# Spectral filter plus MLP on one core: load order, activation table, first tile and schedule changed together

## The chip, the cores and the metric

The kernel runs on one core of one Trainium2 chip. The metric is device time in microseconds, the median of several runs. All times below are in microseconds. The engines are PE (matrix multiply; PEld is its weight load), DVE (vector), ACT (scalar, activation functions), POOL (general) and SP, which here only issues DMAs.

## What is computed

```python
x  = A_x                                   # 1 x 2048 x 640, bf16
xn = (x - mean(x)) / sqrt(var(x) + 1e-5)   # over the last axis
A  = irfft2(rfft2(xn) * (w_r + 1j * w_i))  # filter 2048 x 321
B  = gelu(xn @ w1 + b1) @ w2 + b2          # w1 640 x 1536, w2 1536 x 640, tanh form
return x + A + B
```

## The kernel before

The 2048 rows are 16 tiles of 128 partitions. Both branches start from the normalised rows and meet in one sum at the end.

- **Normalise** (all sixteen tiles): DVE takes two BNStats per tile (L567), an aggregate (mv, L569) and adds epsilon (ve, L571); POOL raises to the power -0.5 (rstd, L572); DVE forms -mean x rstd (nmr, L574) and writes the normalised tile (L595).
- **Transposes**: PE turns each normalised tile with five identity matmuls (L607) into one PSUM bank; DVE or ACT copies it to xnT.
- **First layer**: per block of 1, 1, 2, 2, 2, 4 and 4 tiles and per slice of 128 of the 1536 hidden columns, five matmuls (W by xnT) fill one of the PSUM banks 4 to 7; ACT applies the GELU (L656) and writes gT. W1 is loaded in three parts (W1P).
- **Spectral branch**: DVE folds each pair of tiles (L618, L622), PE multiplies it with gtab, ACT copies to XV; then etab (32- and 128-row matmuls), the small matmuls with mtab, the products with the filter Wf on DVE (T and Z, L723, L727), the small matmuls with ntab, DMA transposes on SP (L748), getab, folds on DVE, htab.
- **Second layer**: per tile 24 matmuls with W2. For the eight tiles in KEEP the second layer is done early into PSUM, DVE adds b2 (b2bc, the bias on all partitions, L824), and POOL adds x by an accumulating DMA (L826). For the others ACT copies b2bc to the place (L803), POOL accumulates x there, and the second layer is summed with the last spectral product in PSUM. DVE adds both and SP writes the tile out (L838).

The order on each engine is made when the program is built: `Sched.schedule` plays all operations against estimated durations (`mm_us`, `dve_us`, `act_us`, `pool_us`) and priorities (`PRIO`), and each engine then runs its list in that order. SP's list was the order of the source. Waits are semaphores; an engine stands at the first instruction of its list whose wait isn't met. `CHAIN` fixes the order of the spectral stages among themselves: b (etab), c (mtab), d (ntab). All DMAs of `load` are issued at L469, and all copies from PSUM to SBUF at L485 (ACT) and L486 (DVE), nearly all matmuls at L474.

SP's list before: x and W1 in pieces with ident, b1t and gtab between them, then etab, mtab, ntab, the 34 filter loads of rows of 642 bytes (Wf), W2, getab, htab, b2bc, then the 16 transposes and the 18 stores. The first part of W1 goes out on ACT's queue.

Of the kernel before, what the change touches and what calls it, by code (L numbers as in the profile page):

```python
# [7 lines left out]
BF = dt.bfloat16  # L8
# [89 lines left out]
def act_us(n, ptr=0):  # L98
    return 0.055 + n / 1200.0 + 0.09 * ptr
# [57 lines left out]
class Sched:  # L157
# [36 lines left out]
    def schedule(self):  # L194
# [24 lines left out]
        while left:  # L219
            best = None  # L220
            for e in self.engines:
# [27 lines left out]
                if e == "sp":  # L249
                    t, o = min(cands, key=lambda c: c[1].seq)  # L250
                    if o is not min((p for p in pend[e] if not p.done), key=lambda p: p.seq):
                        continue
                else:
                    t0 = min(c[0] for c in cands)
                    near = [c for c in cands if c[0] <= t0 + 0.03]
                    if e == "pe" and self.mode != "128":
                        near = [c for c in cands if c[0] <= t0 + HOLD and c[1].alts and c[1].alts[0][0][0] == self.mode] or near
                    t, o = min(near, key=lambda c: (-c[1].prio, c[1].seq))
# [13 lines left out]
            if o.nbytes:  # L272
                if e == "pool":
                    o.end = t + 5.0
                else:
                    s = max(t + 0.9, dma_free)
                    dma_free = s + o.nbytes / o.rate
                    o.end = dma_free + 0.9
            else:
                o.end = t + dur + LAT[e]  # L280
# [96 lines left out]
W1P = [(0, 5), (5, 8), (8, 12)]  # L377
# [5 lines left out]
PRIO = {"hps": 10, "gelu": 50, "pb": 70, "pc": 80, "filt": 85, "ipc": 90, "eps": 60, "fin": 40}  # L383
# [4 lines left out]
HOME = (KEEP[:max(0, len(KEEP) - 7)] + tuple(c for c in range(15) if c not in KEEP))[:8]  # L388
WARM = (55, 12)


def bass_parallel_sum__spectral_gfnet__dense_activation_gelu__prompt_kernel(
# [21 lines left out]
    with ExitStack() as es:  # L414
# [27 lines left out]
        nmr = sb("nmr", [128, 16], F32)  # L442
# [25 lines left out]
        def load(dst, src, buf, nbytes, after=(), reads=(), rate=395e3, q="sp"):  # L468
            return K.op([(q, 0.45)], 400, lambda e, _: e.dma_start(dst, src), reads=reads, writes=[buf], after=after, nbytes=nbytes, rate=rate)  # L469
# [20 lines left out]
        K.op([("dve", 0.1)], 300, lambda e, _: e.memset(warm[:], 0.0), writes=[B_warm])  # L490
        K.op([("pool", 0.1)], 100, lambda e, _: e.memset(mhalf[:], -0.5), writes=[B_mh])
# [16 lines left out]
        def load_x(c, n, q="sp"):  # L508
            o = load(view(X, c * D, [[1, n * D]]), xv[:, c:c + n, :].rearrange("p c d -> p (c d)"), B_x[c], n * D * 256, q=q, rate=155e3 if c == 0 else 395e3)
            for i in range(1, n):  # L510
                B_x[c + i].writers.append(o)

        def load_w1(j, q="sp"):
            a, b = W1P[j]
            load(view(W1, 128 * a, [[F, 5], [1, 128 * (b - a)]]), w1v[:, :, 128 * a:128 * b], B_w1s[j], 163840 * (b - a), q=q, rate=300e3)
# [7 lines left out]
        load_w1(2)  # L523
        load(gtab[:], const["G"], B_g, 524288)
        for c in range(4, 16, 2):
            load_x(c, 2)
        load(etab[:], const["E"], B_e, 204800, rate=250e3)
        load(mtab[:], const["M"], B_m, 65536, rate=70e3)
        load(ntab[:], const["N"], B_n, 49152, rate=70e3)
        WP = 32 * KP  # L530

        def load_w(wsrc, p0, off, row, n, step):
            load(bass.AP(tensor=Wf, offset=p0 * WP + off, ap=[[2 * WP, 16], [2 * KP, n], [1, 321]]),
                 bass.AP(tensor=wsrc.tensor, offset=wsrc.offset + row * 321, ap=[[128 * 321, 16], [step * 321, n], [1, 321]]),
                 B_w, 16 * 642 * n, after=[wpad], rate=165e3)
# [12 lines left out]
        load(W2[:], w2v, B_w2, F * D * 2)  # L548
        load(getab[:], const["GE"], B_ge, 204800)
        load(htab[:].rearrange("p a b -> p (a b)"), const["H"], B_h, 524288)  # L550
        load(b2bc[:], bass.AP(tensor=b2v.tensor, offset=b2v.offset, ap=[[0, 128], [1, D]]), B_b2b, 163840)
# [3 lines left out]
        K.op([("dve", 0.08)], 200, lambda e, _: e.tensor_copy(b1col[:], psb(B_b1ps.slot, [[1, NFC]])), reads=[B_b1ps], writes=[B_b1c])  # L555
# [3 lines left out]
        norm_ops, ring_ops, a_ops = [], [], []  # L559
        B_rs = [Buf(f"rstd{c}") for c in range(16)]  # L560
        for c0, n in [(0, 1), (1, 1)] + [(c, 2) for c in range(2, 16, 2)]:
            pr = 100 - c0 / 2
            B_mv, B_ve, B_r = Buf("mv"), Buf("ve"), Buf("r")
            for c in range(c0, c0 + n):
                B_st = Buf("st")
                for h in range(2):
                    K.op([("dve", 0.393)], pr, lambda e, _, c=c, h=h: e.bn_stats(stats[:, c, 6 * h:6 * h + 6], view(X, c * D + H2 * h, [[1, H2]])),  # L567
                         reads=[B_x[c]], writes=[B_st])
                K.op([("dve", 0.119)], pr, lambda e, _, c=c: e.bn_aggr(mv[:, c, :], stats[:, c, :]), reads=[B_st], writes=[B_mv])  # L569
            a, b = c0, c0 + n  # L570
            K.op([("dve", 0.09)], pr, lambda e, _, a=a, b=b: e.tensor_scalar_add(ve[:, a:b], mv[:, a:b, 1], 1e-5), reads=[B_mv], writes=[B_ve])  # L571
            K.op([("pool", 0.65)], pr, lambda e, _, a=a, b=b: e.tensor_tensor(out=rstd[:, a:b], in0=ve[:, a:b], in1=mhalf[:, a:b], op=ALU.pow),  # L572
                 reads=[B_ve, B_mh], writes=[B_r])
            K.op([("dve", 0.071)], pr, lambda e, _, a=a, b=b: e.scalar_tensor_tensor(out=nmr[:, a:b], in0=mv[:, a:b, 0], scalar=-1.0,  # L574
                                                                                     in1=rstd[:, a:b], op0=ALU.mult, op1=ALU.mult),
                 reads=[B_mv, B_r], writes=B_rs[a:b])
            for c in range(a, b):
                B_rs[c].writers += B_r.writers

        for pair in range(8):  # L580
# [10 lines left out]
            for n in range(2):  # L591
# [4 lines left out]
                    out=xnv(n, 0, [[1, D]]), in0=view(X, c * D, [[1, D]]), scalar1=rstd[:, c:c + 1], scalar2=nmr[:, c:c + 1], op0=ALU.mult, op1=ALU.add),  # L596
                    reads=[B_x[c], B_rs[c]], writes=[xn, B_xn])
                norm_ops.append(o)
                if c in BYDMA:
                    K.op([("sp", 1.6)], 0, lambda e, _, c=c, n=n, xnv=xnv: e.dma_start_transpose(xnT[:, :, 128 * c:128 * c + 128], xnv(n, 0, [[1, D]])),  # L600
                         reads=[B_xn, xn], writes=[B_xnT[c]], nbytes=163840, rate=150e3)
                    continue
                tps = Buf(f"tps{c}", psum, 1, ZONE["tps"])

                def xt(e, _, n=n, xnv=xnv, tps=tps):
                    for j in range(5):
                        ins = e.transpose(psb(tps.slot, [[1, 512]]).bitcast(BF)[:, 128 * j:128 * j + 128], xnv(n, 128 * j, [[1, 128]]), ident[:])  # L607
                    return ins
                tp = K.op([("pe", 5 * mm_us(128))], pr, xt, reads=[B_xn, xn, B_id], writes=[tps], alts=[[("128", 5 * mm_us(128))]])
                if not c:  # L610
                    idle(WARM[1], WARM[1] * mm_us(128), gate=[tp])
                K.op([("dve", 0.41), ("act", act_us(640))], pr,
                     copy(lambda c=c: xnT[:, :, 128 * c:128 * c + 128],
                          lambda tps=tps: psb(tps.slot, [[1, 512]]).bitcast(BF)[:, 0:640].rearrange("p (j t) -> p j t", j=5)),
                     reads=[tps], writes=[B_xnT[c]])
# [54 lines left out]
        def five_segs(n):  # L670
            return [("128", 4 * n * mm_us(Q4)), ("32", n * 0.075 + 0.01)]
# [5 lines left out]
        for gi, (c0, n) in enumerate(GROUPS):  # L677
# [8 lines left out]
            for v in range(2):  # L686
                K.op([("dve", dve_us(320 * n) + 0.05), ("act", act_us(320 * n) + 0.16)], PRIO["pb"] - c0 / 10,
# [3 lines left out]
        for P in range(4):  # L691
# [4 lines left out]
            for r in range(2):  # L696
                cps = Buf(f"cps{P}_{r}", psum, 4, ZONE["cps"])
                zone[f"c{P}{r}"] = pe([("small", 2 * mm_us(KP) + 0.06)], PRIO["pc"] - P / 2 + 0.02 * r, lambda P=P, r=r, cps=cps: [
# [31 lines left out]
            for v in range(2):  # L730
                dps = Buf(f"dps{P}_{v}", psum, 4, ZONE["dps"])
                d_ops.append(pe([("small", 2 * mm_us(H2) + 0.06)], PRIO["ipc"] - P / 2 + 0.02 * (1 - v), lambda P=P, v=v, Zs=Zs, dps=dps: [
# [12 lines left out]
            for pair, U, B_u in zip(two, Us, B_us):  # L745
                for qq in range(2):
                    q = 2 * pair + qq
                    K.op([("sp", 1.3)], 0, lambda e, _, q=q, qq=qq, U=U, uv=uv: e.dma_start_transpose(  # L748
                        XV[:, :, 128 * q:128 * q + 128], uv(U, D * qq, [[1, D]])), reads=[U, B_u], writes=[B_v[q]], nbytes=163840, rate=180e3)
# [11 lines left out]
        for gi, (c0, n) in enumerate(GROUPS):  # L761
# [20 lines left out]
            for i in range(n):  # L782
# [38 lines left out]
                if kept:  # L821
                    kps = Buf(f"kps{c}", psum, 2, ZONE["fps"])
                    second(c, kps, 0, D, pr, ([kept_ops[-2]] if len(kept_ops) > 1 else [pb_ops[0]]) + [l1_of[j][-1] for j, (t0, nt) in enumerate(BLOCKS) if t0 <= c < t0 + nt])
# [4 lines left out]
                for o0, w in [(0, D)] if c < 15 else [(0, H2), (H2, Q4), (H2 + Q4, Q4)]:  # L828
# [9 lines left out]
                    last.append(K.op([("sp", 0.35)], 0, lambda e, _, c=c, os_=os_, o0=o0, w=w: e.dma_start(ov[:, c, o0:o0 + w], view(W1, OST + os_.slot * D + o0, [[1, w]])),  # L838
# [33 lines left out]
```

## Time and profile before

| | before |
|---|---|
| median of 3 runs (lowest to highest) | 157.81 (157.73 to 157.98) |
| profiled execution: span, first to last instruction | 160.8 |
| profiled execution: its own time | only the span is given |
| PE busy | 148.7 (92%) |
| DVE, ACT, POOL busy | 113.2 (70%), 84.0 (52%), 26.2 (16%) |
| mean granted PE clock | 0.979 |
| DMA moved | 21.71 MB, mean 135 GB/s |

The span counts from the first to the last instruction of one execution. Busy shares are averages over stages with different limits. A row of a timeline is: start, length, engine, line, operation, out<-in, shape, count, and in brackets the idle time before it with what ended it. A line that ends in q is the engine's queue of issues.

### The profile page before, as it was taken

How to read it: one execution, taken by the hardware profiler on the slowest of the kernel's cores; microseconds unless marked ns; L12 is line 12 of the kernel's file. 1: busy time of each engine (PE TensorE's matmuls, PEld its weight loads, DVE VectorE, ACT ScalarE, POOL GpSimd, SP SyncE). 2: the span in 40 equal slices, each digit the busy share in tenths (PEclk: the TensorE clock that was granted, in tenths of full speed). 3: DMA queues.
4: the chain of work that ended last, by engine and by line, in shares of the span. 5: the costliest groups of instructions: out<-in, count | busy, mean ns of one | idle time of the engine just before them, and what ended most of it. 6: DMA issues, size and time to landing. Idle time of an engine off the chain costs nothing.

```text
span 160.8 us, 4316 instructions
## 1 busy us (share of the span) xinstructions
PE 148.7 (92%) x1823; PEld 98.4 (61%) x1845; DVE 113.2 (70%) x258; ACT 84.0 (52%) x147; POOL 26.2 (16%) x33
## 2 busy tenths in 40 slices
PE   7979999999981999998999999998999999999994
PEld 7969899999850356464465355443447664665563
DVE  1659999999993024589995786991206999998222
ACT  3288989899709655353246884356865451211000
POOL 1112101111027600302113045202006000000000
PEclk9999999999997589999999999999999999999999
DMA  5999995458941940051649509996651914222112
GB/s 143 356 380 394 212 140 121 105 128 202 378 189 20 207 99 4 4 84 34 131 81 161 90 4 156 208 166 126 138 115 18 167 64 161 86 86 82 41 56 66
DMA packets 30394, 21.71 MB, mean 135 GB/s; under 512 B 12712, under 2 KB 28200, under 8 KB 30376
## 3 DMA queue, kind: packets, MB, share of 16 engines
q1 hardware_dynamic: 23320, 15.39, 38.4%
q0 software_dynamic: 6400, 5.24, 20.2%
q10 hardware_dynamic: 656, 0.82, 1.4%
q8 instruction: 14, 0.23, 0.6%
q14 instruction: 4, 0.03, 0.1%
HBM read 13.58 MB, written 2.62 MB: 101 GB/s over the span
## 4 chain that ended last, share of the span: by engine, by line
PE 57%; SPq 22%; DMA 8%; DVE 4%; ACT 4%; issue 3%; DVEq 0%
PE ps L474 57%; SPq L469 22%; DMA b2bc<-in_B_b_dram 6%; DVE T L723 2%; DMA XV<-U 2%; ACT gT L656 2%; ACT Wf L485 1%; DVE Z L727 1%; ACT xnT L803 1%; DVE Y L486 1%; DVEq L359 0%; ACT U L485 0%; DVE X L824 0%; DVE W L835 0%; SPq L748 0%
## 5 line engine op out<-in xcount | busy, mean ns | idle before, releaser
L474 PE MATMUL ps<-xnT,W 128*128 128x256 bf16 (+2 forms) x413 | 57.8, 294 | 6.0 <-ACT gT L656 4.6
L474 PE MATMUL ps<-W,gT 128*128 128x128 bf16 (+3 forms) x382 | 55.2, 292 | 1.6 <-issue 1.3
L474 PEld LDWEIGHTS ps<-xnT,W 128*128 128x128 bf16 x420 | 35.8, 99 | 23.2 <-ACT gT L656 6.3
L656 ACT ACTIVATE gT<-ps,b1col 128x256 bf16<-128x256 f32 (+2 forms) x84 | 39.7, 506 | 8.8 <-PE ps L474 6.8
L474 PEld LDWEIGHTS ps<-W,gT 128*128 128x128 bf16 x396 | 29.8, 98 | 23.3 <-issue 2.4
L826 POOL DMA_DIRECT2D xnT<-in_A_x_dram x8 | 12.3, 1785 | 33.0 <-ACT xnT L803 23.5
L567 DVE BATCH_NORM_STATS2 stats<-X 128x6 f32<-128x320 bf16 x32 | 14.3, 472 | 2.9 <-DMA X<-in_A_x_dram 2.9
L485 ACT ACTIVATE Wf<-ps 128x960 bf16<-128x960 f32 (+1 forms) x9 | 7.6, 878 | 15.5 <-PE ps L474 15.5
L723 DVE TENSOR_TENSOR T<-Y,Wf 128x1288 bf16<-128x1288 bf16 x16 | 12.4, 821 | 0.8 <-issue 0.8
L572 POOL TENSOR_TENSOR rstd<-ve,mhalf 128x2 f32<-128x2 f32 (+1 forms) x9 | 6.3, 699 | 38.1 <-DVE ve L571 38.1
L485 ACT ACTIVATE Xb<-ps 128x960 bf16<-128x960 f32 (+1 forms) x7 | 7.9, 1157 | 8.0 <-PE ps L474 7.8
L826 POOL DMA_DIRECT2D X<-in_A_x_dram x8 | 7.0, 873 | 27.1 <-DVE X L824 25.6
L485 ACT ACTIVATE XV<-ps 128x1280 bf16<-128x1280 f32 (+1 forms) x8 | 9.3, 1157 | 2.9 <-PE ps L474 2.7
L835 DVE TENSOR_TENSOR W<-ps,xnT 128x640 bf16<-128x640 f32 x8 | 6.5, 819 | 5.6 <-PE ps L474 5.4
L485 ACT ACTIVATE Y<-ps 128x644 bf16<-128x644 f32 x8 | 5.7, 707 | 8.5 <-PE ps L474 8.5
L486 DVE CAST Wf<-ps 128x960 bf16<-128x960 f32 (+1 forms) x3 | 3.1, 1044 | 8.6 <-PE ps L474 8.6
L486 DVE CAST Y<-ps 128x644 bf16<-128x644 f32 x8 | 6.6, 825 | 3.6 <-PE ps L474 3.6
L622 DVE TENSOR_TENSOR T<-T 128x512 bf16<-128x512 bf16 (+1 forms) x32 | 8.5, 315 | 0.0
L486 DVE CAST Xb<-ps 128x960 bf16<-128x960 f32 (+1 forms) x5 | 5.5, 1098 | 4.1 <-PE ps L474 4.1
L485 ACT ACTIVATE U<-ps 128x512 bf16<-128x512 f32 (+1 forms) x12 | 4.6, 435 | 7.1 <-PE ps L474 4.6
L835 DVE TENSOR_TENSOR W<-ps,X 128x640 bf16<-128x640 f32 (+2 forms) x10 | 6.7, 683 | 1.9 <-PE ps L474 1.9
L474 PE MATMUL ps<-getab,XV 32*128 32x160 bf16 (+1 forms) x128 | 7.6, 242 | 0.0
(47 smaller groups left out, 147.7 us busy)
## 6 DMA issues: line engine op xcount, KB each, us to landing
xnT<-in_A_x_dram POOLq DMA_DIRECT2D x8, 320.0 KB, 4.9
X<-in_A_x_dram POOLq DMA_DIRECT2D x8, 320.0 KB, 5.1
out_dram<-W SPq DMA_DIRECT2D x15, 160.0 KB, 1.8
X<-in_A_x_dram SPq DMA_DIRECT2D x7, 320.0 KB, 10.2
W<-in_B_w_dram SPq DMA_DIRECT2D x1, 1920.0 KB, 9.7
Wf<-in_A_w_r_dram SPq DMA_DIRECT2D x15, 80.2 KB, 9.3
Wf<-in_A_w_i_dram SPq DMA_DIRECT2D x15, 80.2 KB, 2.6
W<-in_B_w_dram ACTq DMA_DIRECT2D x1, 800.0 KB, 5.2
```

Of the source, the lines that this page charges most:

```text
L469: return K.op([(q, 0.45)], 400, lambda e, _: e.dma_start(dst, src), reads=reads, writes=[buf], after=after, nbytes=nbytes, rate=rate)
L474: ins = e.matmul(o_, lhsT=lw, rhs=rh, start=st, stop=sp_, skip_group_check=True)
L485: return e.activation(dst(), src(), ACT.Copy, scale=scale)
L486: return e.tensor_copy(dst(), src())
L567: K.op([("dve", 0.393)], pr, lambda e, _, c=c, h=h: e.bn_stats(stats[:, c, 6 * h:6 * h + 6], view(X, c * D + H2 * h, [[1, H2]])), reads=[B ...
L572: K.op([("pool", 0.65)], pr, lambda e, _, a=a, b=b: e.tensor_tensor(out=rstd[:, a:b], in0=ve[:, a:b], in1=mhalf[:, a:b], op=ALU.pow), read ...
L622: ring_ops.append(K.op([("dve", dve_us(4 * w, 2))], pr, lambda e, _, op=op, x1v=x1v, xfv=xfv, o_=o_, o0=o0, o1=o1, w=w: e.tensor_tensor(ou ...
L656: K.op([("act", act_us(128 * nt, 1))], pr + PRIO["gelu"], lambda e, _, c0=c0, nt=nt, fc=fc, hps=hps: e.activation(gT[:, fc, 128 * c0:128 * ...
L723: filt_ops.append(K.op([("dve", dve_us(4 * KP, 2))], pr, lambda e, _, k=k, Y=Y, TB=TB, pair=pair: e.tensor_tensor(out=view(TT, TB.slot * 8 ...
L727: K.op([("dve", dve_us(2 * KP, 2))], pr, lambda e, _, TB=TB, Z=Z, r=r, op=op: e.tensor_tensor(out=view(Zb, Z.slot * 4 * KP + r * KP, [[2 * ...
L826: K.op([("pool", 1.5)], 51, lambda e, _, c=c, xov=xov, shaped=shaped: e.dma_start(xov(0, D), shaped(xv[:, c, :]), accum_op=ALU.add), reads ...
L835: K.op([("dve", dve_us(w))], 95, lambda e, _, os_=os_, fps=fps, o0=o0, w=w, xov=xov, shaped=shaped, base=base: e.tensor_tensor(out=shaped( ...
```

## The change

- Loads: tiles 4 and 5 of x go ahead of gtab. W2 (in two halves), b2bc, and by their place in SP's new list also ntab, getab and htab, stand ahead of the 34 filter loads. SP's list is now made by the scheduler too. W1's parts are 3, 4 and 5 slices instead of 5, 3 and 4; the first still goes out on ACT's queue.
- Activation table: the GELU's table is loaded once, as ACT's first instruction, ahead of its W1 load. Copies use the same table. The copy of b1 to b1col moves from DVE to ACT.
- First tile: its transposes go into two banks, three blocks copied by DVE and two by ACT.
- nmr is gone: the tile is normalised as (x - mean) x rstd.
- Tile 1's first statistics wait in the scheduler for tile 0's normalise to start (its second ones don't, and stand ahead of tile 0's epsilon in DVE's list).
- The scheduler's estimates are changed, the first layer's priority is 45 instead of 10, and the early second layers no longer wait for the first etab matmuls. The order comes out anew: on PE, the transposes of a pair stand around the previous pair's gtab matmuls, 24 second-layer matmuls stand ahead of the first etab ones, first- and second-layer work alternates through the spectral stages, and 42 second-layer with 7 first-layer matmuls stand between the last ntab and the first getab matmuls, where 6 and 35 stood. On POOL, accumulating DMAs stand between the later rstd operations. On ACT, the copies of b2bc begin behind the GELUs of the third block, where they began behind those of the fifth.

```diff
 def act_us(n, ptr=0):
-    return 0.055 + n / 1200.0 + 0.09 * ptr
+    return 0.067 + n / 1200.0 + 0.078 * ptr
...
-                if e == "sp":
-                    t, o = min(cands, key=lambda c: c[1].seq)
-                    if o is not min((p for p in pend[e] if not p.done), key=lambda p: p.seq):
-                        continue
-                else:
...
-W1P = [(0, 5), (5, 8), (8, 12)]
+W1P = [(0, 3), (3, 7), (7, 12)]
...
-PRIO = {"hps": 10, "gelu": 50, "pb": 70, "pc": 80, "filt": 85, "ipc": 90, "eps": 60, "fin": 40}
+PRIO = {"hps": 45, "gelu": 50, "pb": 70, "pc": 80, "filt": 85, "ipc": 90, "eps": 60, "fin": 40}
...
+WLATE = 19.0
...
+        K.op([("act", 1.3)], 410, lambda e, _: e.preload_act_table(ACT.Gelu_apprx_tanh), writes=[Buf("table")])
...
+        load_x(4, 2)
         load(gtab[:], const["G"], B_g, 524288)
-        for c in range(4, 16, 2):
+        for c in range(6, 16, 2):
             load_x(c, 2)
-        load(etab[:], const["E"], B_e, 204800, rate=250e3)
-        load(mtab[:], const["M"], B_m, 65536, rate=70e3)
-        load(ntab[:], const["N"], B_n, 49152, rate=70e3)
+        for h in range(2):
+            load(W2[:, 6 * h:6 * h + 6, :], w2v[:, 6 * h:6 * h + 6, :], B_w2, F * D)
+        load(etab[:], const["E"], B_e, 204800, rate=340e3)
+        load(mtab[:], const["M"], B_m, 65536, rate=200e3)
+        load(b2bc[:], bass.AP(tensor=b2v.tensor, offset=b2v.offset, ap=[[0, 128], [1, D]]), B_b2b, 163840)
+        load(ntab[:], const["N"], B_n, 49152, rate=200e3)
...
-                 B_w, 16 * 642 * n, after=[wpad], rate=165e3)
+                 B_w, 16 * 642 * n, after=[wpad], rate=165e3, issue=0.645, late=WLATE))
...
-        load(W2[:], w2v, B_w2, F * D * 2)
         load(getab[:], const["GE"], B_ge, 204800)
...
-        K.op([("dve", 0.08)], 200, lambda e, _: e.tensor_copy(b1col[:], psb(B_b1ps.slot, [[1, NFC]])), reads=[B_b1ps], writes=[B_b1c])
+        K.op([("act", 0.2)], 200, lambda e, _: e.activation(b1col[:], psb(B_b1ps.slot, [[1, NFC]]), ACT.Copy), reads=[B_b1ps], writes=[B_b1c])
...
-                    out=xnv(n, 0, [[1, D]]), in0=view(X, c * D, [[1, D]]), scalar1=rstd[:, c:c + 1], scalar2=nmr[:, c:c + 1], op0=ALU.mult, op1=ALU.add),
+                    out=xnv(n, 0, [[1, D]]), in0=view(X, c * D, [[1, D]]), scalar1=mv[:, c, 0:1], scalar2=rstd[:, c:c + 1], op0=ALU.subtract, op1=ALU.mult),
...
+                if not c:
+                    st_ops[2].gate.append(o)
...
+                for j0, j1, engs in ((0, 3, ["dve"]), (3, 5, ["act"])) if c == 0 else ((0, 5, ["dve", "act"]),):
+                    nj = j1 - j0
+                    tps = Buf(f"tps{c}", psum, 1, ZONE["tps"])
...
-                    second(c, kps, 0, D, pr, ([kept_ops[-2]] if len(kept_ops) > 1 else [pb_ops[0]]) + [l1_of[j][-1] for j, (t0, nt) in enumerate(BLOCKS) if t0 <= c < t0 + nt])
+                    second(c, kps, 0, D, pr, ([kept_ops[-2]] if len(kept_ops) > 1 else []) + [l1_of[j][-1] for j, (t0, nt) in enumerate(BLOCKS) if t0 <= c < t0 + nt])
```

## The prediction

> **What bounds the kernel now.** I read the table of waits first, then the chain that ended last, then PE's timeline with the clock by stretch, and last the head of ACT's and SP's timelines. The page's own first line says PE is busy 92% of the span, so the question is what the missing time and the slow time of PE are.
>
> Waits (who waited for whom: us in all, times, longest):
>
> ```profile
> PE ps L474 <- ACT gT L656: 4.6, 2, 3.9
> ACT xnT L803 <- DMA b2bc<-in_B_b_dram: 4.4, 1, 4.4
> PE ps L474 <- issue: 1.7, 11, 0.2
> PE ps L474 <- DVE xnT L486: 0.7, 2, 0.5
> ```
>
> One wait of 3.9 us is almost half of all that PE waits after it has started. PE's timeline around it, then four stretches (length; busy time and count on PE, PEld, DVE, ACT, POOL; granted clock; DMA share; GB/s):
>
> ```profile
> 47.14 0.44 PE L607 MATMUL ps<-ident,T 128*128 128x128 bf16 x5
> 51.49 5.73 PE L474 MATMUL ps<-xnT,W 128*128 128x512 bf16 x13 [3.91 <-ACT gT L656]
> 57.02 0.78 PE L474 MATMUL ps<-gtab,T 128*128 128x128 bf16 x10
> ```
> ```profile
> 44.00:48.00 4.00, 3.58 (x32) 2.14 (x30) 3.82 (x13) 0.00 (x0) 0.85 (x1) 1.00 0.55 211
> 48.00:52.00 4.00, 0.51 (x2) 0.23 (x3) 1.54 (x6) 3.65 (x7) 2.62 (x2) 0.79 0.05 8
> 52.00:56.00 4.00, 4.00 (x11) 1.41 (x10) 0.00 (x0) 2.52 (x5) 2.67 (x3) 0.50 1.39 204
> 56.00:60.00 4.00, 3.95 (x35) 2.24 (x34) 0.96 (x1) 2.50 (x4) 0.35 (x1) 0.86 0.61 116
> ```
>
> ACT does nothing from 44 to 48: its queue stands at the copy of b2bc (L803), and the GELUs that would free PE's banks stand behind it. When PE comes back the clock is at half. The SP queue says why b2bc is late:
>
> ```profile
> 9.76 14.78 SPq L469 DMA_DIRECT2D Wf<-in_A_w_r_dram  x17
> 24.57 11.81 SPq L469 DMA_DIRECT2D Wf<-in_A_w_i_dram  x17
> 36.43 0.59 SPq L469 DMA_DIRECT2D W<-in_B_w_dram  x1
> 38.53 0.53 SPq L469 DMA_DIRECT2D b2bc<-in_B_b_dram  x1
> ```
>
> The 34 filter loads take SP 26.6 us to issue; b2bc goes out at 38.5 and lands 9.8 us later. Their own user, the product L723, first runs at 69.1.
>
> The head of ACT:
>
> ```profile
> 0.74 0.46 ACTq L469 DMA_DIRECT2D W<-in_B_w_dram  x1
> 6.89 0.70 ACT L485 ACTIVATE xnT<-ps 128x640 bf16<-128x640 bf16 x1 [4.37 <-PE ps L607]
> 7.92 1.28 ACT L656 ACT_TABLE_LOAD   x1 [0.33 <-DVE b1col L555]
> 9.21 2.42 ACT L656 ACTIVATE gT<-ps,b1col 128x128 bf16<-128x128 f32 x8
> ```
>
> PE starts first-layer work at 7.65, fills its four banks, and waits 0.70 at 9.64 for the GELU behind that table load.
>
> **What of the span can move.** The span is 160.8. PE's useful stream runs from 7.65 to 158.43 with idle of 0.70, 0.47, 0.20, 3.91, 1.7 (eleven small ones), 0.36, 0.49 and 0.28: 8.1 in all. Under the slow clock 13 matmuls of 128x512 took 5.53 (51.49 to 57.02); at 0.216 each (35 of them between 112.50 and 120.06) they are 2.81, so 2.7 is lost, and the ten gtab matmuls behind them took 0.83 where 20.34 to 20.90 shows 0.56: 3.0 in all. Start 7.65, idle 8.1, clock 3.0 and the tail of 2.4 are 21.1; the other 139.7 is matmul streaming, and the change keeps its counts (after and before: 120, 180 and 120 first-layer matmuls of width 128, 256 and 512; 396 second-layer ones).
>
> **Part by part.**
>
> *W2, tables and b2bc ahead of the filter loads.* SP's new order has b2bc 19th, at about 0.74 + 18 x 0.48 = 9.4 us (0.47 each in the first rows of the queue). Ahead of it lie 7.5 MB; the stretches 0:4 to 12:16 moved 141, 356, 380 and 393 GB/s, 5.1 MB by 16 us, and 2.4 MB more at 380 is 6.4 us: it lands near 23. ACT reaches its first L803 after the third block's GELUs; before, the matmuls of that block ended at 25.7, so ACT gets there at about 24.5 in the new time. The wait of 3.9 goes, and with it the clock loss of 3.0. What is late next is PE itself: it streams without idle from 16.6 to 47.6 in the profile. W2 lands near 21 and PE first asks for it behind all 256-wide blocks, past 40.
>
> *The filter loads behind them.* Their issue starts at 22 x 0.48 = 11 instead of 9.8, their data behind all that is ahead of them (about 24.5). The 20:36 stretches carry them at 107 to 139 GB/s, so 2.6 MB at 120 is 22 us: about 47. The first product is due near 61. Cost nothing; cover 14 us; past that each us is a us. The transposes that SP issues behind them (81.05 before) are later still.
>
> *One table load, first on ACT.* The 1.28 at 7.92 leaves the path. But it now stands ahead of ACT's issue of the first W1 part, which moves from 0.74 to about 2.05; that part shrinks from 800 to 480 KB (landing 5.2 us after issue before), so it lands between 5.5 and 7.0, before the first matmul. Price if not: up to 1 us. The bias copy goes to ACT ahead of xnT's copy and waits on b1t's DMA, issued 2.13: covered until 6.6.
>
> *First tile.* Chain before: statistics at 3.65, ve at 4.81, rstd 5.05, nmr 5.66, normalise 5.85, transposes 6.41. The new order drops nmr (0.2) but puts a BNStats of tile 1 (0.4) ahead of ve: normalise near 6.05. That one waits for tile 1's x, which landed at 6.5 before; with W1 off the engines until 2.05 it should be there by 4.8. Copies: DVE's three blocks stand behind a BNStats and an aggregate (0.5), so both end near 7.45. Gain there 0 to 0.2. GELU starts near 8.0 instead of 9.21, and the idle of 0.70, 0.47 and 0.20 is gone, less 0.2 for W1's third part, landing near 11 and needed near 11.3. Together 1.2.
>
> *nmr elsewhere, W1 split, copies moved to ACT:* DVE loses 7 x 0.08 and gains one XV copy (about 1.1), gives two xnT copies (0.4 each) to ACT: nothing, as PE is the full engine there.
>
> *New order in the middle.* The two old waits (0.36, 0.49) go with their places. New: the third xb copy now stands on DVE behind the first products. In the rows the first Y copy after its matmuls starts 0.17 later, DVE then spends 67.54 to 69.10 on its semaphore waits for the filter loads, and the products and sums take 0.75 each. From the matmul's end that copy ends at 0.17 + 0.8 + 1.6 + 4 x 0.75 + 2 x 0.4 + 1.2 = 7.5 us; PE's fill until it needs it (20 matmuls of 0.216, 24 etab at 1.31 in all, 6 of W2 at 0.136) is 6.5. New wait 1.0; net +0.15.
>
> *Ahead of getab.* From the end of the last but two inverse matmuls (105.5) SP needs 0.9 to start, 12.6 for eight transposes (106.40 to 119.0) and some 1.5 to land: 15.0. PE had 15.4 of work there; the new order leaves 25 x 0.216 + 60 x 0.136 + 2 x 0.44 = 14.4. Cost 0.6 (0 to 1.5).
>
> *All other places of the new order:* nearest rows are the waits of 0.36 and 0.49; from -0.5 to 2; I take 0.5.
>
> Sum: -3.9 - 3.0 - 1.2 + 0.15 + 0.6 + 0.5 = -6.85: a span of 153.95.
>
> **From the span to the median.** The median is 3.0 under the profiled span. Streaming at full clock can't be shorter, so in the timed runs the 21.1 is at most 18.1. I spread that evenly: -6.85 x 18.1/21.1 = -5.9, 151.9. If all 3.0 is missing in the very stall and its clock, the gain is 3.85 and the time 154.0; if none is, 151.0.
>
> On that clock: the rows show 0.79, 0.50 and 0.86 after a wait of 3.91 us. The Trainium skill (TensorE: Matmul & The Clock Gate, Part 1) says the gate falls to half after an idle window of about 3.4 us, and that the window runs free of the kernel. By it a 3.9 us wait is near the edge, and the timed runs may hold the wait without the slow clock; the gain would then lie 3.0 lower.
>
> On the table: the row has the GELU at 9.21, where the load ends at 9.20. The skill (ScalarE: Activation LUTs, What ACT_TABLE_LOAD costs) adds a drain of 1.38 to each load, 2.66 together. By it the part would bring up to 1.4 more; this trace shows no drain.
>
> **Rivals.**
> 1. *The timed runs hold little of the stall.* For: the 3.0 between span and median, as large as the clock's 3.0. Against: the three runs lie within 0.25, so no chance state. Time 153.5 to 156.
> 2. *b2bc still ends last, slower.* ACT stands at its first L803 with all GELUs behind it; POOL has its first accumulating DMA ahead of the next rstd, so DVE's normalise stops too. Price: one us for each us past 24.5, and 3.0 of clock once the wait is as long as the 3.9 of before. Over the old time from a landing past about 30, that is with 7.5 MB at under 270 GB/s. Against: 356 to 393 in the rows. Time 158 to 161.
> 3. *The head turns bad:* W1's first part behind the table load comes after 7.5, or the BNStats stands waiting for x. Costs 1 to 1.5 and gives 153.5.
> 4. *The new order's waits fall away* (priced 2.1 with the small places): 150.
>
> **How the numbers follow.** Forecast, 150.6 to 153: 0.48. Rivals 1 and 3, 153 to 156: 0.32. Rival 4, below 150.6: 0.10. Rival 2: 0.07; no change at all 0.03. The range 150.0 to 155.8 leaves out rival 2, no change and the edges of 1 and 4. About 0.2% is what a measurement can tell from no change here. Faster 0.90, same 0.02, slower 0.08.
>
> **What would show it.** Right: no wait of ACT for b2bc; no stretch with clock under 1.0 after the start; one table load; first GELU near 8.0; PE's stream ending near 152 in the profile; short waits (about 1 and 0.6) at the third xb and ahead of getab. Wrong: a wait of DVE L725 for Wf, of POOL's rstd behind its DMAs, PE idle over 2 us anywhere, or a DVE that ends last between 45 and 65.

## The result and the profile after

The change is slower: 159.79 (158.41 to 160.70, twelve runs) against 157.81 (156.94 to 160.37, twelve runs) for the kernel before; ratio 1.0115, interval 1.0085 to 1.0145. The forecast was 151.9 (150.0 to 155.8). The profiled run took 159.97 with a span of 158.2, so 1.77 lies around the span. The runs after fall into two groups by mean granted clock, five at 1.00 (median 158.54) and seven at 0.989 (159.6 to 160.7, the profiled run among them), and the five are 1.0 above the nine runs at clock 1.00 in which the kernel before was timed again (median 157.58).

The page, first line and the rows of PE and its clock in 40 slices; then who waited for whom on PE (us in all, times, longest):

```profile
span 158.2 us, 4332 instructions
...
PE   7699999999999999999999999999749899999993
...
PEclk9999999999999999999999999999978999999999
```
```profile
PE ps L469 <- DMA XV<-U: 2.5, 1, 2.5
PE ps L608 <- DVE T L591: 1.3, 1, 1.3
...
PE ps L469 <- DVE Wf L481: 0.7, 1, 0.7
PE ps L469 <- DVE X L826: 0.5, 1, 0.5
PE ps L469 <- DVE Xb L481: 0.4, 1, 0.4
```

The stall at 48 us is gone, and its hole in the PE row. A new one stands in the 29th and 30th slices, and the clock falls in the 30th and 31st: PE waits 2.5 us for the last DMA transposes ahead of getab. PE's timeline there, and two stretches (columns as ahead of the prediction):

```profile
112.39 1.80 PE L469 MATMUL ps<-W,gT 128*128 128x512 bf16 x12 [0.49 <-DVE X L826]
116.72 1.71 PE L469 MATMUL ps<-getab,XV 128*128 128x160 bf16 x16 [2.52 <-DMA XV<-U]
118.36 2.63 PE L469 MATMUL ps<-W,gT 128*128 128x512 bf16 x12
120.82 1.37 PE L469 MATMUL ps<-getab,XV 128*128 128x160 bf16 x24
```
```profile
112.00:116.00 4.00, 1.80 (x12) 0.88 (x12) 0.34 (x1) 1.88 (x3) 3.31 (x3) 1.00 1.23 178
116.00:120.00 4.00, 3.28 (x23) 2.01 (x24) 1.42 (x3) 0.70 (x1) 0.58 (x1) 0.58 1.12 164
```

The DMA share in both stretches is above 1.1. SP's queue shows the transposes that PE waits for. POOL's timeline shows what else was issued then: four accumulating DMAs of 320 KB (tiles 10, 11, 13 and 14).

```profile
107.10 2.53 SPq L750 DMA_TRANSPOSE XV<-T  x2
109.67 4.11 SPq L750 DMA_TRANSPOSE XV<-U  x2
```
```profile
108.28 0.86 POOL L828 DMA_DIRECT2D X<-in_A_x_dram  x1 [4.49 <-DVE X L826]
112.63 0.86 POOL L828 DMA_DIRECT2D X<-in_A_x_dram  x1 [3.50 <-DVE X L826]
113.55 3.03 POOL L828 DMA_DIRECT2D xnT<-in_A_x_dram  x2
```

For the transposes issued from 104 to 120 us, the trace gives this time from issue to landing:

```profile
DMA to landing us min/median/max: 2.6/5.0/6.2
```

In the same window of the kernel before, in which POOL issued one such DMA, it was 2.6/2.7/4.3.

### The profile page after: what moved, and what is told of

It is laid out like the page before. It is cut to its first block, busy times and chain, and to the rows that moved or that the text cites. A ratio compares the mean times of both kernels' runs of the same rounds, so it can differ in the third digit from the quotient of the medians.

```text
span 158.2 us, 4332 instructions
## 1 busy us (share of the span) xinstructions
PE 148.9 (94%) x1845; PEld 97.1 (61%) x1845; DVE 115.0 (73%) x251; ACT 79.9 (51%) x145; POOL 26.4 (17%) x33
## 4 chain that ended last, share of the span: by engine, by line
PE 80%; DMA 6%; DVE 5%; SPq 3%; ACT 3%; issue 1%; DVEq 0%; POOL 0%
PE ps L469 77%; DMA XV<-U 3%; SPq L750 3%; PE ps L608 3%; DMA X<-in_A_x_dram 2%; DVE T L725 2%; ACT Wf L480 1%; ACT XV L480 1%; DVE Xb L481 1%; DVE Wf L481 1%; DVE Z L729 1%; SPq L464 1%; ACT T L480 0%; DVEq L354 0%; POOL rstd L573 0%
## 5 line engine op out<-in xcount | busy, mean ns | idle before, releaser
L469 PE MATMUL ps<-W,gT 128*128 128x512 bf16 (+3 forms) x396 | 58.6, 298 | 0.5 <-DVE X L826 0.5
L469 PE MATMUL ps<-xnT,W 128*128 128x256 bf16 (+2 forms) x420 | 57.0, 288 | 0.2 <-ACT gT L658 0.2
L469 PEld LDWEIGHTS ps<-W,gT 128*128 128x128 bf16 x396 | 30.4, 99 | 25.1 <-issue 3.2
L469 PEld LDWEIGHTS ps<-xnT,W 128*128 128x128 bf16 x420 | 34.6, 98 | 15.3 <-issue 1.7
L480 ACT ACTIVATE Wf<-ps 128x960 bf16<-128x960 f32 (+1 forms) x9 | 7.6, 880 | 21.1 <-PE ps L469 21.1
L568 DVE BATCH_NORM_STATS2 stats<-X 128x6 f32<-128x320 bf16 x32 | 14.9, 474 | 3.4 <-DMA X<-in_A_x_dram 3.4
L480 ACT ACTIVATE Xb<-ps 128x960 bf16<-128x960 f32 (+1 forms) x6 | 6.8, 1135 | 6.7 <-PE ps L469 6.7
L469 PEld LDWEIGHTS ps<-getab,XV 32*128 32x128 bf16 (+1 forms) x128 | 6.8, 147 | 5.0 <-DMA XV<-U 2.9
L481 DVE CAST Xb<-ps 128x960 bf16<-128x960 f32 (+1 forms) x6 | 6.7, 1122 | 4.2 <-PE ps L469 4.2
L480 ACT ACTIVATE XV<-ps 128x1280 bf16<-128x1280 f32 (+1 forms) x7 | 8.0, 1145 | 3.4 <-PE ps L469 3.4
L826 DVE TENSOR_TENSOR X<-ps,b2bc 128x640 f32<-128x640 f32 x7 | 5.7, 818 | 4.8 <-PE ps L469 4.8
L608 PE MATMUL ps<-ident,T 128*128 128x128 bf16 x80 | 7.1, 220 | 1.3 <-DVE T L591 1.3
```

The lines of the kernel that those rows point to most:

```text
L469: ins = e.matmul(o_, lhsT=lw, rhs=rh, start=st, stop=sp_, skip_group_check=True)
L480: return e.activation(dst(), src(), ACT.Copy, scale=scale)
L481: return e.tensor_copy(dst(), src())
L568: st_ops.append(K.op([("dve", 0.393)], pr, lambda e, _, c=c, h=h: e.bn_stats(stats[:, c, 6 * h:6 * h + 6], view(X, c * D + H2 * h, [[1, H2 ...
L826: kept_ops.append(K.op([("dve", dve_us(D))], 30, lambda e, _, kps=kps, xov=xov, shaped=shaped: e.tensor_tensor(out=xov(0, D), in0=shaped(p ...
```

## The experiments

There were two theories. One: the stall and the slow clock that the first profile shows are larger than in most runs, so moving the loads was worth little. Two: the new order lets POOL's accumulating DMAs fall on the last transposes, and the wait with its slow clock eats the gain. The rival to the second was that the mere number of matmuls ahead of getab is too small.

Every ratio is against the kernel before as it was timed beside the run. That was done three times: its medians were 157.75 beside the first four runs recorded (the kernel before again, the loads alone, the DMAs held, more matmuls), 158.05 beside four others (only the later DMAs held, and the three on the head) and 158.12 beside the last two (idle matmuls, the loads back). So a difference of 0.3 between runs of two of these groups shows nothing by itself.

### The kernel before, again

No edit.

> The kernel before, unchanged, to see the span and the granted clock of each of its timed runs. Theory A (the profile that the prediction rested on was a bad execution): most timed runs have a clock of 1.0 and a span of 155 to 156.5, some 5 under the profiled 160.8, since a run with the whole wait for b2bc also has the slow clock. Rival B (the timed runs hold the whole wait, and the profiled span is only longer by what profiling adds): clock 0.98 in every run and spans of 160 to 161.

Measured: 157.66 (156.97 to 159.84, twelve runs). Nine have spans of 155.2 to 156.6 at clock 1.00, three of 158.0 to 158.1 at 0.989. PE's and SP's timelines of its profile, span 155.8:

```profile
49.24 3.15 PE L474 MATMUL ps<-xnT,W 128*128 128x512 bf16 x13 [1.15 <-ACT gT L656]
...
54.30 0.97 PE L474 MATMUL ps<-etab,XV 128*128 128x160 bf16 x16
```
```profile
9.50 11.99 SPq L469 DMA_DIRECT2D Wf<-in_A_w_r_dram  x17
21.54 12.86 SPq L469 DMA_DIRECT2D Wf<-in_A_w_i_dram  x17
...
36.59 0.43 SPq L469 DMA_DIRECT2D b2bc<-in_B_b_dram  x1
```

The wait is 1.15 instead of 3.91, and the 13 matmuls behind it run at full clock (3.15 instead of 5.73). The filter loads took 24.9 to issue instead of 26.6, so b2bc went out 1.9 earlier. Of the 5.0 between the two spans, 4.84 lie ahead of the first etab matmuls (54.30 against 59.14). The first profile had even begun its first-layer matmuls 0.5 sooner (7.65 against 8.15), so the stall and its clock differ by some 5.3. With 1.8 around the span, as in the profiles whose time is known, the first profile's execution took an estimated 162.6, more than the slowest timed run of this kernel in any comparison (160.97): it was an outlier in the very place that the change mends.

### The loads alone

Before, with only W2 and b2bc moved ahead of the filter loads in SP's list; all other orders kept.

```diff
         K.schedule()
+        sp = K.order["sp"]
+        early = [o for o in sp if o.name in ("w2", "b2")]
+        sp[:] = [o for o in sp if o not in early]
+        at = [o.name for o in sp].index("W")
+        sp[at:at] = early
         K.sync()
```

> The kernel before with one thing changed: W2 and b2bc stand ahead of the 34 filter loads in SP's list; the order on every other engine is kept as it was. Theory A: only what is left of the wait in the timed runs goes, 1.5 to 2.5, so 155.3 to 156.3. Rival B: the wait of 3.9 and the clock loss of 3.0 go, 151.

Measured: 155.50 (155.15 to 155.75, six runs), ratio 0.9877 (0.985 to 0.9903), clock 1.00 in each. PE's timeline at the old stall:

```profile
47.38 2.98 PE L474 MATMUL ps<-xnT,W 128*128 128x512 bf16 x13
...
52.27 0.97 PE L474 MATMUL ps<-etab,XV 128*128 128x160 bf16 x16
```

No wait is left; etab starts 2.03 earlier than in the run above, of which 0.54 was there before any load that moved could matter (first first-layer matmul at 7.61 against 8.15). In the median the load move is worth 2.2. All six runs are at clock 1.00, where three of twelve above were not; six runs are few, and only suggest that the lower clock goes with the stall.

### POOL's last DMAs held

After, with POOL's last four accumulating DMAs waiting for the last two transposes (`turned` collects the transposes; where it is filled is not shown). This is the held kernel below.

```diff
         K.schedule()
+        for o in K.order["pool"]:
+            if o.name in ("xo10", "xo11", "xo13", "xo14"):
+                o.deps = o.deps + turned[-2:]
         K.sync()
```

> The changed kernel with one thing changed: POOL's last four accumulating DMAs (tiles 10, 11, 13, 14) wait until the last two transposes have landed; all orders are kept. Theory A (those DMAs share the engines with the last transposes and make PE wait ahead of getab): the last transpose lands about 2.6 after its issue instead of 5.0, PE's wait of 2.5 ahead of getab falls under 0.7, the clock is 1.0 in every run, the time 155.5 to 157. Rival C (the fill of 14.4 us ahead of getab is too short by itself, since SP issues the transposes one by one): the wait stays over 1.5 and the time over 158.

Measured: 155.97 (155.70 to 156.25, six runs), ratio 0.991 (0.9882 to 0.9938), clock 1.00 in each. PE, SP and POOL, and the landing of the transposes in the same window:

```profile
112.31 1.80 PE L469 MATMUL ps<-W,gT 128*128 128x512 bf16 x12 [0.49 <-DVE X L827]
113.95 1.04 PE L469 MATMUL ps<-getab,XV 128*128 128x160 bf16 x16
114.92 1.80 PE L469 MATMUL ps<-W,gT 128*128 128x512 bf16 x12
116.56 1.37 PE L469 MATMUL ps<-getab,XV 128*128 128x160 bf16 x24
```
```profile
109.58 3.00 SPq L751 DMA_TRANSPOSE XV<-U  x2
```
```profile
114.15 1.75 POOL L829 DMA_DIRECT2D X<-in_A_x_dram  x2 [10.45 <-DMA XV<-U]
```
```profile
DMA to landing us min/median/max: 2.6/3.6/4.5
```

With the same matmuls ahead of getab the wait is gone, so it was not their number. It was the DMAs: 3.8 in the median. In the two profiles the first getab matmuls start 2.8 later in the change (116.72 against 113.95; 0.1 of it comes from earlier places), the second ones 4.3 later (120.82 against 116.56), and PE's last matmul is still 4.2 later: some 2.7 for the wait, 1.5 for the slow clock behind it, and nothing after that. Both the last two issues on SP (4.11 against 3.00) and the landing behind them (2.9 against at most 1.4) are shorter without the DMAs; which of the two is the first cause the runs do not separate. The Trainium skill (DMA: Bandwidth & Descriptors, Issuing engines are not separate DMA queues) says that DMAs started by ScalarE, SyncE or GpSimd run on the same 16 engines and interleave; these runs agree.

### Only the later DMAs held

The held kernel, with tile 10's DMA at 108.3 left free. Those of tiles 13 and 14 stand behind tile 11's in POOL's list and so wait with it.

```diff
-            if o.name in ("xo10", "xo11", "xo13", "xo14"):
+            if o.name == "xo11":
```

> The held kernel, but only the last three accumulating DMAs (tiles 11, 13, 14, issued after the last transpose in the change's profile) wait for the transposes; tile 10's, issued between them at 108.3, goes out as in the change. If the one in between makes the transposes late, PE waits 1.5 or more ahead of getab again and the time is over 157.5; if the later three do it, it is near 156.0.

Measured: 157.37 (156.90 to 157.58, twelve runs), ratio 0.9989 (0.9963 to 1.0015); clock 0.999 or 1.00 in each.

```profile
115.50 1.07 PE L469 MATMUL ps<-getab,XV 128*128 128x160 bf16 x16 [1.25 <-DMA XV<-U]
```

Half of the wait comes back with this one DMA, between the two forecasts. It costs 1.4 in the median (157.37 - 155.97), or 1.1 when each is taken from the kernel before timed beside it. The later three make up the rest, some 2.4, of which the next run shows the clock's part.

### The wait filled with idle matmuls

After, with 50 matmuls of zeros behind the last second-layer matmul ahead of getab, so that PE is busy while it waits.

```diff
...
+            for _ in range(50):
+                ins = e.matmul(psb(bank, [[1, 128]], 768), lhsT=warm[:], rhs=warm[:], start=True, stop=True, skip_group_check=True)
...
```

> The changed kernel with 50 idle matmuls (2.8 us of PE, into unused columns of a bank) ahead of the first getab matmuls, where PE waits for the last transposes; all else kept. Theory (the wait itself costs 2.5, and the slow clock behind it another 1.5 in those runs that have it): the wait is covered, not shortened, the clock is 1.0 in every run and all times lie at 158.2 to 159.0, without the ones near 160. Rival (the slow clock comes from elsewhere): clock 0.989 in about half of the runs still.

Measured: 158.59 (158.49 to 159.17, ten runs), ratio 1.0058 (1.0025 to 1.0091); clock 0.999 or 1.00 in each.

```profile
113.91 2.96 PE L851 MATMUL ps<-warm 128*128 128x128 bf16 x50
116.78 1.07 PE L469 MATMUL ps<-getab,XV 128*128 128x160 bf16 x16
```

getab starts no earlier (116.78 against 116.72), and runs in 1.07 instead of 1.71. The time is that of the change's own runs at clock 1.00. So the lower clock in seven of the twelve runs follows the idle wait, and costs about 1.5 there (159.97 against 158.5).

### More matmuls ahead of getab

After, with the first layer's old priority and with the early second layers waiting for the first etab matmuls as before. From this the scheduler makes another order, with 32 first-layer and 6 second-layer matmuls there.

```diff
-PRIO = {"hps": 45, ...
+PRIO = {"hps": 10, ...
-... ([kept_ops[-2]] if len(kept_ops) > 1 else []) + ...
+... ([kept_ops[-2]] if len(kept_ops) > 1 else [pb_ops[0]]) + ...
```

> The changed kernel with the first layer's priority at 10 again and the early second layers behind the first etab matmuls again; the scheduler then puts 32 first-layer and 6 second-layer matmuls ahead of getab (7.7 us) where the change has 7 and 42 (7.2). Theory A and rival C: no wait ahead of getab, since fewer accumulating DMAs fall there and the fill is longer: 154.5 to 156.5, clock 1.0. Rival D (the loss is spread over the small waits of the new order, not at getab): under 1 better than the change.

Measured: 157.04 (155.36 to 160.71, twelve runs), ratio 0.9951 (0.9912 to 0.9989); clock 1.00 in ten, 0.979 and 0.989 in two. The expected time and clock were missed. There is no wait ahead of getab: POOL issues no accumulating DMA from 102.4 to 115.9, and the transposes from 104 to 120 land after 2.6 in the median. But a new wait stands earlier, which the trace puts down to nothing that it shows:

```profile
100.61 2.32 PE L469 MATMUL ps<-xnT,W 128*128 128x512 bf16 x10 [1.55 <-issue]
```

The order moves too much at once to tell theory A from rival C. It shows only that the order of the change is not the best that this scheduler makes.

### The head: statistics, table, and the two parts that gain

First, the held kernel with tile 1's second statistics also behind tile 0's normalise in DVE's list:

```diff
+        dve = K.order["dve"]
+        dve.remove(st_ops[3])
+        dve.insert(dve.index(norm_ops[0]) + 1, st_ops[3])
```

> The held kernel (last four accumulating DMAs behind the transposes) with one thing changed in DVE's list: tile 1's second statistics stand behind tile 0's normalise, not ahead of tile 0's epsilon. The change's profile shows DVE idle 0.73 for tile 1's x there, and the first first-layer matmul at 8.14 against 7.64 before. Theory: it starts near 7.35 and the gain of 0.7 to 0.8 stays to the end, as PE streams from there on: 155.2. Rival: GELU on ACT paces the head, or the transposes ahead of getab take it back: under 0.3.

Measured: 155.58 (155.03 to 155.88, six runs), ratio 0.9874 (0.9829 to 0.9918), 0.4 under the held kernel, or 0.7 when each is taken from the kernel before timed beside it. The first first-layer matmul starts at 7.34 instead of 8.05; whether any of these 0.7 is lost again later is not shown.

Second, the held kernel with the table of the copies loaded first, so that the GELU's load stands ahead of the first GELU again:

```diff
-e.preload_act_table(ACT.Gelu_apprx_tanh)
+e.preload_act_table(ACT.Copy)
```

> The held kernel with the copies' table loaded first instead of the GELU's, so that the second load stands ahead of the first GELU again; all orders kept. Theory: the first GELU comes 1.28 later, PE's four banks run full, and 0.8 to 1.3 is lost: 156.8 to 157.3. Rival (the transposes or DVE pace the head, so the table is free): under 0.3 lost.

Measured: 156.76 (156.25 to 156.82, twelve runs), ratio 0.9939 (0.9913 to 0.9965), 0.8 over the held kernel, or 0.5 when each is taken from the kernel before timed beside it. ACT's timeline:

```profile
8.03 1.28 ACT L658 ACT_TABLE_LOAD   x1
9.32 2.92 ACT L658 ACTIVATE gT<-ps,b1col 128x128 bf16<-128x128 f32 x9
```

The load is on the path for less than its own 1.28: the first GELU stands 0.8 later than in the held kernel (9.32 against 8.53). It starts as the load ends.

Third, the kernel before with both parts that gain, the load move (as above, not shown again) and the one table, and all its other orders:

```diff
+        K.op([("act", 0.0)], 410, lambda e, _: e.preload_act_table(ACT.Gelu_apprx_tanh), writes=[Buf("table")])
...
+        act = K.order["act"]
+        act.insert(0, act.pop([o.name for o in act].index("table")))
...
```

> The kernel before with W2 and b2bc ahead of the filter loads and the GELU's table loaded once at the start; every order kept. Theory: PE's wait of 0.70 for the first GELUs goes, tile 1's transposes and copy come that much sooner, and 0.5 to 0.8 of it stays: 154.8. Rival (DVE paces the head): same as with the loads alone, 155.5. It shows what the two useful parts of the change are worth without its new order.

Measured: 154.76 (median of six, five of them 154.51 to 155.16 and one of 379.35, whose cause is not known), ratio 0.983 (0.9783 to 0.9877). It beats both kernels. ACT's timeline:

```profile
7.83 2.04 ACT L657 ACTIVATE gT<-ps,b1col 128x128 bf16<-128x128 f32 x7 [0.55 <-DVE ve L572]
```

The first GELU stands at 7.83, against 9.18 with the loads alone, and PE's wait of 0.70 for it is gone. It gains 0.7 over the loads alone, or 1.0 when each is taken from the kernel before timed beside it.

### The loads back, in the new order

After, with W2 and b2bc behind the filter loads again:

```diff
+        late = [o for o in sp if o.name in ("w2", "b2")]
+        sp[:] = [o for o in sp if o not in late]
+        at = max(i for i, o in enumerate(sp) if o.name == "W") + 1
+        sp[at:at] = late
```

> The changed kernel with W2 and b2bc put back behind the 34 filter loads in SP's list; every other order kept. It prices the rival that b2bc still ends last. ACT stands at its first copy of b2bc at about 25; before, b2bc landed near 45 in its usual runs, and the GELUs stand behind that copy. Theory: PE waits from about 27 until b2bc lands near 43 to 47, 15 to 20 with the slow clock behind it, so 174 to 182. Rival (POOL, DVE and PE have enough other work in that stretch): under 5 lost.

Measured: 176.29 (two runs, 176.21 and 176.37), ratio 1.1173 (1.1118 to 1.1228). The table of waits:

```profile
DVE T L591 <- POOL rstd L573: 18.1, 3, 16.7
ACT xnT L805 <- DMA b2bc<-in_B_b_dram: 18.1, 1, 18.1
PE ps L469 <- ACT gT L658: 17.2, 2, 17.0
```

ACT stands 18.1 us for b2bc, POOL and DVE behind it, and PE 17.0, and the time is 16.5 above the change: the price of about one us for each us that rival 2 named is real. The new order needs the moved loads.

## Why the prediction was wrong

Scaled by 18.1/21.1 as in the prediction, its steps were -5.9 for the stall and its clock, -1.0 for the head and +1.1 for the new order. The runs gave -2.2, -0.7, +1.2 (155.97 - 154.76: the held kernel against loads and table, which has the rest of the head in it) and +3.8 for the DMAs on the transposes. These four are steps along one chain of runs from the kernel before to the change, so their sum of +2.1 proves nothing; only the split is found by experiment, good to some 0.3 where it joins runs of two groups. Of the 7.9 by which 151.9 fell short, about 7.0 are two steps of nearly equal size, 3.7 and 3.3.

**From the span to the median** put the stall and its clock 3.7 too high (5.9, measured 2.2). The 3.0 between span and median was spread evenly over 21.1. The gap was 4.8, as the 1.8 around the span were not counted, and nearly all of it lay in the one stall and its clock. Rival 1 named this: the stall and its clock at 6.9, less the 3.0, are 3.9, and less the 4.8 they are 2.1, close to what was measured. The argument against it, that three close runs exclude chance, said nothing of the profiled execution, whose span alone (160.8) was longer than any of the three times.

**Ahead of getab** was priced 0.6 (0.5 when scaled), with 1.5 as its upper bound, and cost 3.8: a wait of 2.52, and 1.5 of clock behind it in seven of twelve runs. What failed is the transposes' own time. The prediction added 0.9, 12.6 and 1.5 from the end of the last but two inverse (ntab) matmuls to the last landing, 15.0 in all. In the change these took 1.0, 14.1 and 2.9, 17.9 in all (98.76 to 116.67). In the held kernel the same transposes had landed within 15.3 (98.68 to 113.95), and PE's work covered them: but for the DMAs, the step's count was right. The chain of waits of after:

```profile
109.67 1.98 SPq L750
...
111.69 4.98 DMA XV<-U
...
116.72 5.50 PE ps L469 x52
```

The last two issues took 4.11 together, 1.1 more than in the held kernel, and the last transpose landed 2.9 after they ended (116.67 - 113.78). Where POOL's four DMAs fall in the new order, beside the transposes, has no term in the sum: their cost was put at nothing without a reason. "PE idle over 2 us anywhere" was named as what would prove the prediction wrong, and did.

**The loads**, as a mechanism, held. SP's and ACT's timelines of after:

```profile
11.60 3.91 SPq L464 DMA_DIRECT2D etab<-c_E  x1
...
16.03 0.87 SPq L464 DMA_DIRECT2D b2bc<-in_B_b_dram  x1
...
18.37 12.27 SPq L464 DMA_DIRECT2D Wf<-in_A_w_r_dram  x17
```
```profile
25.09 0.73 ACT L805 ACTIVATE xnT<-b2bc 128x640 f32<-128x640 bf16 x1
```

b2bc was issued at 16.0, not 9.4, because the issue of W2 and etab stalled; it landed at 24.0 (23 predicted), and ACT's copy at 25.1 did not wait. The first product came at 60.81 (61 predicted) without a wait for Wf.

**The head** gained, but less. ACT's and DVE's timelines of after:

```profile
0.74 1.28 ACT L486 ACT_TABLE_LOAD   x1 [0.74 <-PEq L859]
0.77 0.44 ACTq L464 DMA_DIRECT2D W<-in_B_w_dram  x1
...
8.62 1.20 ACT L658 ACTIVATE gT<-ps,b1col 128x128 bf16<-128x128 f32 x4 [0.57 <-PE ps L469]
```
```profile
5.43 0.49 DVE L568 BATCH_NORM_STATS2 stats<-X 128x6 f32<-128x320 bf16 x1 [0.73 <-DMA X<-in_A_x_dram]
...
6.67 0.45 DVE L591 TENSOR_SCALAR T<-X,mv,rstd 128x640 bf16<-128x640 bf16 x1 [0.70 <-POOL rstd L573]
```

W1's issue was not late (0.77, predicted 2.05). The statistics of tile 1 did wait for x, 0.73, and the normalise came at 6.67 instead of 6.05: the half of rival 3 that was seen, worth 0.4 to 0.7 in the statistics run. The first GELU stood at 8.62 (8.0 predicted).

**The third xb copy** was priced 1.0 and made PE wait 0.37. The other new places, put at 0.5, are the waits of 0.49 and 0.71 in the table of waits.

## What to carry to other kernels

Before a wait in a profile is priced, that execution is to be put beside the timed runs, with the time around the span added: if it is slower than all of them, ask which wait the difference sits in; here nearly all of it sat in the largest one. When an order changes, it is not enough to count the work that covers a wait; list the DMAs of every engine that will be in flight at the place, since an accumulate of 320 KB lengthened the wait for a transpose by over 1 us. And parts of a change that gain are best tried without the reorder that came with them: loads and table alone were about 3% faster than the whole (154.76 against 159.79).

## What was not expected of the hardware

- **A wait of 2.52 us is enough for half clock, in some runs.** Behind it the granted clock was 0.58 over four us of the profile (0.50 from 117 to 120), and seven of twelve runs have a mean of 0.989; with the wait filled, none of ten does. Waits of 1.15, 1.25 and 1.55 left the profiles that show them at 1.00. Why only some runs fall is not shown. The Trainium skill (TensorE: Matmul & The Clock Gate, Part 1) puts the idle window at about 3.4 us and lets it run free of the kernel; that the same kernel falls on either side agrees, that 2.52 us suffices does not follow from it, and the measurement decides.
- **A table load does not hold back a DMA issue of its own engine:** the load runs from 0.74 to 2.02, W1's issue on ACT's queue starts at 0.77.
- **No drain behind a table load is seen:** in the run with two tables 8.03 + 1.28 is 9.31, and the GELU starts at 9.32. The Trainium skill (ScalarE: Activation LUTs, What ACT_TABLE_LOAD costs) adds 1.38 for it; the second load cost 0.5 to 0.8 in all.
- **SP's issues took many times longer while the DMAs were full:** the issue of two halves of W2 took 3.66 and that of etab 3.91, where the single loads ahead of them took 0.4 to 0.6 each; the core moved about 400 GB/s then (412 and 401 in the third and fourth slices of the page). With the loads alone moved, the issue of b2bc took 8.15.
